# A dynamic convolution ahead of an FFN: one PSUM quadrant per head in the conv, with the last two heads spread by DMA

## The chip, the cores and the metric

The kernel runs on one core of a Trainium2 chip. The metric is the device time of one execution in microseconds (us); lower is better. For the kernel before, three runs gave 747.69, 746.68 and 747.04 us, a median of 747.04 us.

## What is computed

`x` has 8 batches of 4096 tokens with 192 channels; `weight_gen` has 8 heads of 7 taps for each token. The softmax of the taps weighs the token and the six before it, head by head (24 channels each). The result goes through an FFN with a squared ReLU: 192 to 2048 to 192.

```python
w = softmax(weight_gen, axis=-1)                    # B, S, H=8, K=7
x_unf = x_pad[:, idx, :].reshape(B, S, K, H, 24)    # token s-6 .. s
y = einsum('bshk,bskhg->bshg', w, x_unf).reshape(B * S, 192)
h = maximum(y @ w_in, 0.0)                          # 192 x 2048
out = (h * h) @ w_out                               # 2048 x 192
```

## The kernel before

**Blocks.** The 32768 tokens are cut into 64 sub-blocks of 512 tokens (`TB`), and these into 33 blocks (`BLOCKS`): two of one sub-block, then 31 of two. The two halves of a block stand in partitions 0 to 63 and 64 to 127 of `y`, so that matmuls of 64 rows for the two halves lie beside each other in the array.

**Softmax (class `Softmax`).** ACT does the exponentials (step E, L217). DVE sums, inverts and scales them in pieces of eight rows, or six for a last piece (step S: L224, L231, L239), into `v_first` or `v_big`. From there the weights go to rows `wr`, either by DMAs within SBUF on SP and POOL in turn (`move_rows`, `wr_load_sbuf`, L330) or through DRAM (`store` L253, `wr_load`). `TIMES` and the rule beside it say in which block and ahead of which unit each piece is done. From block 4 to block 26 every block has a piece ahead of its last unit, u15; every fourth has another ahead of u9.

**Bands (`st_bands`, L348, step B).** DVE multiplies `wr` by a mask into `bd`, a banded matrix for each head: 128 input tokens by up to 104 output tokens. In steady blocks the two sub-blocks' bands stand ahead of u1 and u5; in blocks 4 to 6 they stand ahead of u7 and u9, or u5 and u9.

**Conv (`st_conv`, step C).** The conv of block j+1 runs within block j. For five token tiles of a sub-block, a piece of `x` (128 tokens by up to 32 channels) is the stationary operand and `bd` of one head the moving one. The 192 channels are six groups of 32 (`quads`), two to a slot `k`; a half has two column groups of 32 in PSUM. A group of 32 channels covers parts of two heads (24 channels each), so it takes two matmuls: all 32 columns with the later head, then the first 8, 16 or 24 again with the earlier head. That makes 3 slots x 2 x 5 tiles x 2 halves x 2 groups = 120 matmuls for a block of two. Two ACT copies (L432), of 1024 and 512 columns, take the two PSUM tiles `yp` to `y` in f16.

**FFN.** A unit u (`st_unit`, 16 in a block) is six h matmuls (L446), a ReLU on ACT into `t1` (L455) and a square on DVE into `g` (L458). The weights `w_i` lie in SBUF twice: as loaded, and with the halves of 64 rows exchanged. A step M (`st_mm2`, L480) is half of a quarter of the second matmul of the block before: M1 of a block uses g0 to g7 and M2 uses g8 to g15 of the block before, both for its first quarter. After every second M, ACT and DVE add the two halves of `o` into `o_sb` (L494, L496), and SP stores it.

**Order.** It is written out by hand. Each engine runs its instructions in program order. Blocks 0 to 3 have plans of their own, the others follow `steady`: eight M, sixteen u and one C. What has a due time (E, S, B, L) is put ahead of its unit. After the conv of block j+1, POOL issues the loads of `x` for block j+2 (`x_load`, L290, L294, L300), into the two buffers that the conv has just read. `h` of a unit and `yp` share three PSUM buffers of two banks (`ps_h`); `t1` has five buffers, `g` 28, `y` two.

Of the kernel before, what the change touches and what calls it, by code (L numbers as in the profile page):

```python
# [9 lines left out]
def kernel(  # L10
# [26 lines left out]
    nc = tc.nc  # L37
    f32 = mybir.dt.float32
    f16 = mybir.dt.float16

    B, S, D = x.shape
    H, KK = weight_gen.shape[2], weight_gen.shape[3]
    Dff = moe_w_in.shape[1]
    Dm = moe_w_out.shape[1]
    HK = H * KK
    HP = H // 2

    P = 128
    TB = 512
    NBB = S // TB  # L50
    NSUB = B * NBB
    BLOCKS = [(0, 1), (1, 1)] + [(n, 2) for n in range(2, NSUB, 2)]
# [6 lines left out]
    RT = 64  # L59
    NK = D // RT  # L60

    NT = 5
    STEP = 104
    BASE = -24
    starts = [BASE + STEP * i for i in range(NT)]
    bounds = [0, 104, 208, 312, 416, TB]
# [5 lines left out]
    const = ctx.enter_context(tc.tile_pool(name="const", bufs=1))  # L72
# [6 lines left out]
    p_y = ctx.enter_context(tc.tile_pool(name="p_y", bufs=2))  # L79
# [4 lines left out]
    ps_h = ctx.enter_context(tc.tile_pool(name="ps_h", bufs=3, space=bass.MemoryType.PSUM))  # L84
# [3 lines left out]
    WQ = 2  # L88
    NQ = Dff // WQ
    w_i = const.tile([P, WQ, 2, NQ + NQ // 2], f16, name="w_i")  # L90
    w_o = const.tile([P, NF, Dm], f16, name="w_o")
    mask = const.tile([P, P, 2], f16, name="mask")
    swap = const.tile([P, P], f16, name="swap")
    FIRST = 8
    PARTS = {0: (8, 8, 8, 8), 1: (8, 8, 16), 2: (16, 16)}
    v_big = const.tile([P, R + 2 * HALO, HP, SL, 2], f16, name="v_big")
    v_first = [
        const.tile([P, FIRST + 2 * HALO, HP, SL, 2], f16, name=f"v_first{i}") for i in (0, 1)
    ]
# [47 lines left out]
                )  # L147
            nc.scalar.copy(out=w_i[:, q, 1, a:b], in_=pt[:, 0 : b - a])

    def w_in_chunk(fc, slot, half):  # L150

        q, f = divmod(fc, NQ // P)
        if slot < 2:
            part, col = slot, f * P
        else:
            second, f = divmod(f, NQ // P // 2)
            part, col = int(second != half), NQ + f * P
        return w_i[RT * half : RT * (half + 1), q, part, col : col + P]
# [10 lines left out]
    class Softmax:  # L169
# [10 lines left out]
        def load(self, eng):  # L180
            r, rh = self.r, self.rh
            self.wg = wg = self.tile(p_wg, p_wg, "wg", HK, "wg8").rearrange(
                "p (r h k) -> p r h k", h=H, k=KK
# [4 lines left out]
            def src(first, count, parts):  # L188
                return bass.AP(
                    tensor=base.tensor, offset=base.offset + first * HK,  # L190
                    ap=[[r * HK, parts], [1, count * HK]],
                )
# [12 lines left out]
        def exp(self, lo, hi):  # L205

            if lo == 0:
                self.ex = self.tile(p_one, p_one, "ex", HK, "ex8").rearrange(
                    "p (r g k e) -> p r g k e", g=HP, k=KK, e=2
                )  # L210
# [57 lines left out]
    x_t, wr_t, bd_t, yp_t, y_t, g_t, h_t, t1_t, o_t, o_sb_t = ({} for _ in range(10))  # L268

    def rows(ap2d, t0, width):  # L270

        return bass.AP(
            tensor=ap2d.tensor, offset=ap2d.offset + t0 * width,
            ap=[[width, P], [STEP * width, NT], [1, width]],
        )
# [5 lines left out]
    def tile_start(j, i):  # L281

        t1 = (j % NBB + 1) * TB
        return TB - P if i == NT - 1 and t1 in ends(j // NBB) else starts[i]
# [17 lines left out]
    def x_load(j):  # L302
        x_t[j] = p_x.tile([P, NT, D], f16, name="xt")
        block_load(j, x_t[j], x[j // NBB], D, nc.gpsimd)

    def x_load_f32(j):
        x_st[j] = p_one.tile([P, (R + HALO) * HK], f32, name="x_st", tag="ex")
        block_load(
# [51 lines left out]
            op=AluOp.mult,  # L360
        )

    G = D // H
    quads = []
    for q in range(D // 32):
        ha, hb = (32 * q) // G, (32 * q + 31) // G
# [3 lines left out]
    def conv_pieces(j):  # L370
# [18 lines left out]
        else:  # L389
            for pair in zip(*halves):  # L390
                for later in (True, False):
                    for k in range(NK):
                        for s, i, half, a, b, base in pair:
                            for q in (2 * k, 2 * k + 1):
                                yield later, s, i, q, half, a, b, base

    def st_conv(j):

        n = BLOCKS[j][1]
        th = n * TB // 2  # L400
        per = 1024 // th
        y = p_y.tile([P, NK, TB], f16, name="y")
        y_t[j] = y
        yps = [
            ps_h.tile([P, 2 * TB], f32, name="yp", tag="h") for _ in range(-(-NK // per))
        ]
        for later, s, i, q, half, a, b, base in conv_pieces(j):
            lo = bounds[i]
            hi = lo + (STEP if tile_start(s, i) == starts[i] else bounds[i + 1] - lo)
            _, ha, hb, pre = quads[q]  # L410
            m, h = (32, hb) if later else (pre, ha)
            bd = bd_t[s][:, H * lo : H * hi].rearrange("p (g c e) -> p g e c", g=HP, e=2)
            p0 = RT * half + 32 * (q % 2)
            k = q // 2
            col = th * (k % per) - base
            nc.tensor.matmul(  # L416
                out=yps[k // per][p0 : p0 + m, col + a : col + b],
                lhsT=x_t[s][:, i, 32 * q : 32 * q + m],
                rhs=bd[:, h // 2, h % 2, a - lo : b - lo],
                start=True,  # L420
                stop=True,
                skip_group_check=True,
                tile_position=(0, p0),
            )
        for n, yp in enumerate(yps):
            k0, k1 = n * per, min((n + 1) * per, NK)

            copies = ((k0, k1, nc.scalar.copy),)
            if j == 0:
                copies = ((0, 2, nc.scalar.copy), (2, NK, nc.vector.tensor_copy))  # L430
            for a, b, copy in copies:
                copy(  # L432
                    out=y[:, a:b, 0:th],
                    in_=yp[:, (a - k0) * th : (b - k0) * th].rearrange("p (k c) -> p k c", c=th),
                )

    def st_unit(j, u):

        th = BLOCKS[j][1] * TB // 2
        per = TB // th  # L440
        h = ps_h.tile([P, 2, TB], f32, name="h", tag="h")
        for jj in range(per):
            for slot in range(NK):
                for half, r0 in enumerate((0, RT)):
                    k = slot ^ half if slot < 2 else slot
                    nc.tensor.matmul(  # L446
                        out=h[:, half, jj * th : (jj + 1) * th],
                        lhsT=w_in_chunk(u * per + jj, slot, half),
                        rhs=y_t[j][r0 : r0 + RT, k, 0:th],
                        start=(jj == 0 and slot == 0), stop=(slot == NK - 1),  # L450
                        skip_group_check=True,
                        tile_position=(r0, 0),
                    )
        t1 = p_t1.tile([P, 2, TB], f16, name="t1")
        nc.scalar.activation(out=t1, in_=h, func=ActF.Relu)  # L455
        g = p_g.tile([P, 2, TB], f16, name="g")
        g_t[(j, u)] = g
        nc.vector.tensor_tensor(out=g, in0=t1, in1=t1, op=AluOp.mult)  # L458
# [56 lines left out]
    with nc.allow_low_precision("fp16 matmul pipeline"), tc.manual_schedule():  # L515
# [26 lines left out]
        def spin(n):  # L542
# [3 lines left out]
        s0, s1, s2 = parts[:3]  # L546
# [5 lines left out]
        w_st = [  # L552
            p_wg.tile([P, (R + HALO) * HK], f32, name="w_st", tag="wg")[:, 0 : NQ + NQ // 2]
            for q in (0, 1)
# [23 lines left out]
        for q in range(4):  # L578
# [4 lines left out]

        steady = "MuMuuu" * 3 + "MuuuMCu"
        plans = {
# [4 lines left out]
        }  # L592


# [28 lines left out]
        for n, s in enumerate(parts[4:], 4):  # L623
            b, f = s.b, s.fb
            k = n - min(m for m, p in enumerate(parts) if p.b == b)
# [8 lines left out]
        for j in range(len(plans), NBLK - 1):  # L634
            a = BLOCKS[j + 1][0]
# [4 lines left out]
        for j in range(len(plans), NBLK):  # L640
            plan, u = [], 0
# [55 lines left out]
        for j in range(NBLK):  # L697
            if j + 2 < NBLK:
                load_rows(j + 2)
            u = 0  # L700
            for step in plans[j].split():
                kind, n = step[0], int(step[1:] or 0)
                if kind == "u":
                    st_unit(j, u)
                    u += 1
                elif kind == "M":
                    next(mm2)
                elif kind == "C" and j + 1 < NBLK:
                    st_conv(j + 1)
                    if j == 0:  # L710
                        x_load(3)
                    elif j + 2 < NBLK:
                        for k in range(BLOCKS[j + 2][0], sum(BLOCKS[j + 2])):
                            x_load(k)
                elif kind == "E":
                    parts[n].exp(*next(parts[n].exps))
                elif kind == "S":
                    soft(parts[n])
                elif kind == "B":
                    st_bands(n)  # L720
                elif kind == "L":
                    parts[n].load(nc.sync)
                elif kind == "X":
                    x_cast(n, nc.vector.tensor_copy)


        j = NBLK - 1
# [44 lines left out]
```

The softmax here doesn't subtract the row's maximum and nothing guards it: scores larger than these inputs give would overflow.

## Time and profile before

| what | value |
|---|---|
| three runs | 747.69, 746.68, 747.04 us; median 747.04 us |
| the profiled execution: span from first to last instruction | 746.6 us (0.4 us under the median of the runs) |
| its own time outside the span | not given by the page; taken as that 0.4 us |
| granted TensorE clock over the span | 1.000 |
| h matmuls (L446), one | 370 ns mean, 3168 of them |
| o matmuls (L480), one | 243 ns mean, 8032 of them |
| conv matmuls (L416), one | 208 ns mean, 3864 of them |
| ReLU (L455), one | 1026 ns, 512 of them |
| square (L458), one | 687 ns, 512 of them |

A row of the page's groups gives line, engine, operation, operands, count, busy time and the mean of one. Matmuls overlap, so the mean of one is longer than the distance from one to the next; distances between starts in the timeline are what counts. The chain is followed back from the last instruction to whatever released it. A wait names the engine that idled and what ended it.

### The profile page before, as it was taken

What the parts mean: (1) busy time and instruction counts of PE and PEld (TensorE: products, weight loads), DVE (VectorE), ACT (ScalarE), POOL (GpSimd) and SP (SyncE); (2) the same over time, 40 slices, a digit from 0 to 9 for tenths busy, and PEclk for the clock granted to TensorE, in tenths of its full rate; (3) what the DMA queues carried; (4) which work ended last, traced back from release to release, by engine and by line L of the source; (5) the groups of instructions that cost most, each with busy time, mean ns of one, the idle gap of its engine ahead of it and who ended that gap; (6) DMA issues with size and microseconds to landing.
All of it is one profiled execution on the core that took longest, in us unless ns stands there. A gap on an engine that the chain in (4) does not pass through costs nothing.

```text
span 746.6 us, 33289 instructions
## 1 busy us (share of the span) xinstructions
PE 738.7 (99%) x15106; PEld 556.1 (74%) x15106; DVE 621.7 (83%) x1002; ACT 624.4 (84%) x755; POOL 89.3 (12%) x130
## 2 busy tenths in 40 slices
PE   8999999999999999999999999999999999999998
PEld 4767777777777778777877777777778777777787
DVE  5999998998889888887889888898888987677853
ACT  4998888898888888888888888888888888888884
POOL 7322220101101100011000110001100011000000
PEclk9999999999999999999999999999999999999999
DMA  7745444436554234643245442265341354432312
GB/s 214 121 97 119 80 86 99 99 72 139 94 118 80 73 59 80 139 79 73 40 80 139 94 72 56 48 139 108 59 80 46 59 108 80 60 70 52 53 46 65
DMA packets 122169, 64.81 MB, mean 87 GB/s; under 512 B 83849, under 2 KB 118636, under 8 KB 121516
## 3 DMA queue, kind: packets, MB, share of 16 engines
q1 hardware_dynamic: 77708, 45.66, 22.3%
q0 software_dynamic: 44176, 16.93, 20.5%
q8 instruction: 118, 1.93, 1.1%
q14 instruction: 23, 0.19, 0.1%
q10 hardware_dynamic: 144, 0.10, 0.0%
HBM read 48.61 MB, written 28.70 MB: 104 GB/s over the span
## 4 chain that ended last, share of the span: by engine, by line
PE 91%; DVE 4%; DMA 2%; ACT 2%; issue 1%; DVEq 0%; ACTq 0%; SPq 0%
PE o L480 43%; PE h L446 42%; PE yp L416 6%; DVE bd L348 2%; DVE g L458 1%; ACT t L455 1%; DMA vd<-v_big 1%; DMA wr<-v_first 1%; DMA wg<-in_weight_gen_dram 0%; DVE v_big L239 0%; ACT ex L217 0%; DVE o_sb L496 0%; DVE ssum L224 0%; DVE rcp L231 0%; DVE v_first L239 0%
## 5 line engine op out<-in xcount | busy, mean ns | idle before, releaser
L455 ACT ACTIVATE t<-h 128x1024 f16<-128x1024 f32 x512 | 496.7, 1026 | 64.5 <-PE h L446 63.9
L458 DVE TENSOR_TENSOR g<-t 128x1024 f16<-128x1024 f16 x512 | 334.1, 687 | 99.1 <-ACT t L455 96.4
L480 PEld LDWEIGHTS <-g 64*128 64x128 f16 (+1 forms) x8032 | 352.5, 94 | 54.2 <-issue 3.8
L480 PE MATMUL o<-w_o,g 64*128 64x192 f16 (+1 forms) x8032 | 385.4, 243 | 0.2
L446 PE MATMUL h<-y,w_i 64*128 64x512 f16 (+1 forms) x3168 | 380.3, 370 | 1.9 <-ACT t L455 0.8
L446 PEld LDWEIGHTS <-w_i 64*128 64x128 f16 x3168 | 162.5, 94 | 117.5 <-issue 5.2
L348 DVE TENSOR_TENSOR bd<-wr,mask 128x4160 f16<-128x4160 f16 (+3 forms) x89 | 149.3, 1701 | 4.2 <-DMA wr<-v_first 4.2
L300 POOL DMA_DIRECT2D xt<-in_x_dram x62 | 51.6, 836 | 445.6 <-PE yp L416 422.7
L494 ACT COPY o_sb<-o 128x384 f32<-128x384 f32 x129 | 62.2, 482 | 33.7 <-PE o L480 33.7
L496 DVE TENSOR_TENSOR o_sb<-o,o_sb 128x384 f32<-128x384 f32 x123 | 68.2, 554 | 8.2 <-ACT o_sb L494 5.6
L432 ACT CAST y<-yp 128x1024 f16<-128x1024 f32 (+1 forms) x64 | 47.9, 799 | 15.1 <-PE yp L416 15.0
L416 PE MATMUL yp<-bd,xt 128*32 128x104 f16 (+8 forms) x3864 | 52.0, 208 | 0.7 <-DVE bd L348 0.3
L416 PEld LDWEIGHTS <-xt 128*32 128x32 f16 (+3 forms) x3864 | 46.2, 92 | 7.1 <-issue 6.4
L239 DVE TENSOR_TENSOR v_big<-ex,rcp 128x112 f16<-128x112 f32 (+1 forms) x136 | 27.3, 264 | 2.1 <-DMA vd<-v_big 0.9
L217 ACT ACTIVATE ex<-wg 128x448 f32<-128x448 f32 (+2 forms) x44 | 27.2, 618 | 2.1 <-DMA wg<-in_weight_gen_dram 2.1
L224 DVE TENSOR_REDUCE ssum<-ex 128x64 f32<-128x448 f32 (+2 forms) x44 | 26.1, 593 | 2.6 <-ACT ex L217 2.6
L231 DVE RECIPROCAL rcp<-ssum 128x64 f32<-128x64 f32 (+2 forms) x44 | 23.7, 539 | 1.5
L290 POOL DMA_DIRECT2D xt<-in_x_dram x7 | 3.8, 548 | 137.1 <-PE yp L416 137.1
L330 POOL DMA_DIRECT2D wr<-v_first x31 | 16.8, 559 | 16.1 <-DVE v_first L239 15.9
L544 PE MATMUL wp<-warm 128*128 128x512 f16 x39 | 10.7, 440 | 1.3 <-DVE warm L536 1.3
L544 PEld LDWEIGHTS <-warm 128*128 128x128 f16 x39 | 4.2, 111 | 7.1 <-issue 2.6
L239 DVE TENSOR_TENSOR v_first<-ex,rcp 128x112 f16<-128x112 f32 (+1 forms) x48 | 9.1, 255 | 0.3
(25 smaller groups left out, 28.7 us busy)
## 6 DMA issues: line engine op xcount, KB each, us to landing
out_dram<-o_sb SPq DMA_DIRECT2D x63, 384.0 KB, 3.0
xt<-in_x_dram POOLq DMA_DIRECT2D x42, 240.0 KB, 6.2
wg<-in_weight_gen_dram SPq DMA_DIRECT2D x4, 1064.0 KB, 8.3
xt<-in_x_dram POOLq DMA_DIRECT2D x20, 192.0 KB, 5.4
wr<-vd SPq DMA_DIRECT2D x38, 80.0 KB, 3.9
vd<-v_big SPq DMA_DIRECT2D x5, 512.0 KB, 5.5
wg<-in_weight_gen_dram SPq DMA_DIRECT2D x5, 392.0 KB
wg<-in_weight_gen_dram SPq DMA_DIRECT2D x3, 616.0 KB, 4.5
```

The costliest lines, as they stand in the source:

```text
L217: nc.scalar.activation(out=self.ex[:, lo:hi].rearrange("p r g k e -> p (r g) k e"), in_=self.wg[:, lo:hi].rearrange("p r (g e) k -> p (r g ...
L239: eng.tensor_tensor(out=bass.AP(tensor=v.tensor, offset=v.offset + lo * H * SL + lo % SL * 2 + g * SL * 2, ap=[list(v.ap[0]), [H * SL + 2, ...
L300: eng.dma_start(out=dst[:, first:last], in_=ap)
L348: nc.vector.tensor_tensor(out=bd_t[j][:, H * lo : H * (lo + len(tiles) * n)].rearrange("p (g m c) -> p g m c", g=shape[1], c=2 * SL), in0= ...
L416: nc.tensor.matmul(out=yps[k // per][p0 : p0 + m, col + a : col + b], lhsT=x_t[s][:, i, 32 * q : 32 * q + m], rhs=bd[:, h // 2, h % 2, a - ...
L432: copy(out=y[:, a:b, 0:th], in_=yp[:, (a - k0) * th : (b - k0) * th].rearrange("p (k c) -> p k c", c=th),)
L446: nc.tensor.matmul(out=h[:, half, jj * th : (jj + 1) * th], lhsT=w_in_chunk(u * per + jj, slot, half), rhs=y_t[j][r0 : r0 + RT, k, 0:th], ...
L455: nc.scalar.activation(out=t1, in_=h, func=ActF.Relu)
L458: nc.vector.tensor_tensor(out=g, in0=t1, in1=t1, op=AluOp.mult)
L480: nc.tensor.matmul(out=oo[:, cc * Dm : (cc + 1) * Dm], lhsT=g[r0 : r0 + n, cc * P : (cc + 1) * P], rhs=w_o[r0 : r0 + n, fc, :], start=(fc ...
L494: nc.scalar.copy(out=o_sb, in_=o[0][:, c])
L496: nc.vector.tensor_tensor(out=o_sb, in0=o[1][:, c], in1=o_sb, op=AluOp.add)
```

## The change

From block 4 on, `st_conv` goes to a new function, `st_conv_spread`. Each head has a column group of 32 of its own: heads 0 to 5 in slots 0 to 2, heads 6 and 7 in a fourth slot. All weights have 32 columns; the eight beyond a head's 24 are channels of a neighbour that are not wanted there. A matmul per head suffices: 4 slots x 5 tiles x 2 halves x 2 = 80. The slots are computed in the order 3, 2, then 0, 1, each pair in one `yp`, copied by ACT with 1024 columns. Then four DMAs on SP, one for each group of 32 partitions, take the 24 rows of the fourth slot into the eight unused rows of each of the first three slots. The rows of `y` thereby come in another order, and the FFN's first weights are loaded a second time in that order, as `w_p`, by 18 DMAs on POOL during block 0. Units of blocks from 4 on use `w_p`. The conv stands earlier in the plan of block 3 and of every later block.

```diff
+    G = D // H
+    SPREAD = H - 2
+    FIRST_SPREAD = 4
...
+    w_p = const.tile([P, WQ, 2, NQ + NQ // 2], f16, name="w_p")
...
+    def load_w_spread():
+
+        def rows(head, k=None):
+            a = moe_w_in[G * head : G * (head + 1)]
+            return a if k is None else a.rearrange("(r k) c -> k r c", k=NK)[k]
+
+        for e in (0, 1):
+            for k in range(NK):
+                for a, n, src in (
+                    (0, G, rows(2 * k + e)), (G, RT // 2 - G, rows(SPREAD + e, k))
+                ):
+                    if k < 2:
+                        p0 = RT * k + 32 * e + a
+                        nc.gpsimd.dma_start(
+                            out=w_p[p0 : p0 + n, :, 0, 0:NQ],
+                            in_=src.rearrange("r (q c) -> r q c", q=WQ),
+                        )
+                    else:
+                        for half in (0, 1):
+                            p0 = RT * half + 32 * e + a
+                            nc.gpsimd.dma_start(
+                                out=w_p[p0 : p0 + n, :, 0, NQ:],
+                                in_=src.rearrange("r (q h c) -> h r q c", q=WQ, h=2)[half],
+                            )
+        for r0, r1 in ((0, RT), (RT, 0)):
+            nc.gpsimd.dma_start(out=w_p[r0 : r0 + RT, :, 1], in_=w_p[r1 : r1 + RT, :, 0])
...
+    def st_conv_spread(j):
+
+        s0, n = BLOCKS[j]
+        y = p_y.tile([P, NK + 1, TB], f16, name="y")
+        y_t[j] = y
+        for ks in ((NK, NK - 1), (0, 1)):
+            yp = ps_h.tile([P, 2, TB], f32, name="yp", tag="h")
+            k0 = min(ks)
+            for k in ks:
+                for i in range(NT):
+                    a, b = bounds[i], bounds[i + 1]
+                    for half in (0, 1):
...
+                        for e in (0, 1):
+                            head = 2 * k + e
+                            p0 = RT * half + 32 * e
+                            c0 = min(G * head, D - 32)
+                            nc.tensor.matmul(
+                                out=yp[p0 : p0 + 32, k - k0, a:b],
+                                lhsT=x_t[s][:, i, c0 : c0 + 32],
+                                rhs=bd[:, head // 2, e, 0 : b - a],
+                                start=True,
+                                stop=True,
+                                skip_group_check=True,
+                                tile_position=(0, p0),
+                            )
+            nc.scalar.copy(out=y[:, k0 : k0 + 2], in_=yp)
+        for p0 in range(0, P, 32):
+            head = SPREAD + p0 // 32 % 2
+            r0 = p0 + G * head - min(G * head, D - 32)
+            nc.sync.dma_start(out=y[p0 + G : p0 + 32, 0:NK], in_=y[r0 : r0 + G, NK])
+
     def st_conv(j):
 
+        if j >= FIRST_SPREAD:
+            return st_conv_spread(j)
...
+        w = w_p if j >= FIRST_SPREAD else w_i
...
-                        lhsT=w_in_chunk(u * per + jj, slot, half),
+                        lhsT=w_in_chunk(w, u * per + jj, slot, half),
...
-        steady = "MuMuuu" * 3 + "MuuuMCu"
+        steady = "MuMuuu" * 2 + "MuMuu" + "MCuu" + "Muuu"
...
-            3: "L5 L6 M S3 u u u M u u u u M u M B6 E4 u u u M M B7 u u u E4 M u M C S4 u",
+            3: "L5 L6 M S3 u u u M u u u u M u M B6 E4 u u u M M B7 u u C u E4 M u M S4 u",
...
                     st_conv(j + 1)
                     if j == 0:
                         x_load(3)
+                        load_w_spread()
```

More of the change, by code (lines that the diff above doesn't have):

```diff
@@ L148, in cross_w_in_by_pe, with w_in_chunk @@
             nc.scalar.copy(out=w_i[:, q, 1, a:b], in_=pt[:, 0 : b - a])
-    def w_in_chunk(fc, slot, half):
+    def load_w_spread():
[22 more added lines that the diff above has]
+            nc.gpsimd.dma_start(out=w_p[r0 : r0 + RT, :, 1], in_=w_p[r1 : r1 + RT, :, 0])
+    def w_in_chunk(w_i, fc, slot, half):
         q, f = divmod(fc, NQ // P)
@@ L361, in st_band @@
         )
-    G = D // H
     quads = []
@@ L395, in conv_pieces @@
                                 yield later, s, i, q, half, a, b, base
+    def st_conv_spread(j):
[9 more added lines that the diff above has]
+                    for half in (0, 1):
+                        s = s0 + half
+                        hi = a + (STEP if tile_start(s, i) == starts[i] else b - a)
+                        bd = bd_t[s][:, H * a : H * hi].rearrange(
+                            "p (g c e) -> p g e c", g=HP, e=2
+                        )
[11 more added lines that the diff above has]
+                                tile_position=(0, p0),
+                            )
+            nc.scalar.copy(out=y[:, k0 : k0 + 2], in_=yp)
[3 more added lines that the diff above has]
+            nc.sync.dma_start(out=y[p0 + G : p0 + 32, 0:NK], in_=y[r0 : r0 + G, NK])
     def st_conv(j):
+        if j >= FIRST_SPREAD:
+            return st_conv_spread(j)
         n = BLOCKS[j][1]
```

## The prediction

> **What bounds the kernel now.** I read the page first (busy shares, then the chain), then the timeline around one conv, then the waits, then windows from conv to conv.
>
> ```profile
> PE 738.7 (99%) x15106; PEld 556.1 (74%) x15106; DVE 621.7 (83%) x1002; ACT 624.4 (84%) x755; POOL 89.3 (12%) x130
> ...
> PE 91%; DVE 4%; DMA 2%; ACT 2%; issue 1%; DVEq 0%; ACTq 0%; SPq 0%
> ```
>
> TensorE (PE) is busy throughout and holds 91% of the chain; from about 145 us on, the windows from conv to conv are 22.5 to 22.9 us each, wholly PE, with DVE at 18.5 to 22.0 us and ACT at 19.1 to 20.0 us. So a matmul taken out is time gained, unless PE is then made to wait. One conv and what follows it (start, duration, engine):
>
> ```profile
> 415.97 1.43 PEld L416 LDWEIGHTS <-xt 128*32 128x32 f16 x120 [0.16 <-issue]
> 415.97 1.59 PE L416 MATMUL yp<-bd,xt 128*32 128x104 f16 x120
> ...
> 416.35 0.69 DVE L458 TENSOR_TENSOR g<-t 128x1024 f16<-128x1024 f16 x1 [0.22 <-ACT t L455]
> ...
> 417.15 1.50 ACT L432 CAST y<-yp 128x1024 f16<-128x1024 f32 x2 [0.46 <-PE yp L416]
> 417.43 0.49 DVE L224 TENSOR_REDUCE ssum<-ex 128x48 f32<-128x336 f32 x1
> ...
> 417.50 0.82 PE L446 MATMUL h<-y,w_i 64*128 64x512 f16 x6
> ...
> 418.15 1.48 PE L480 MATMUL o<-w_o,g 64*128 64x192 f16 x32
> 418.44 0.71 DVE L239 TENSOR_TENSOR v_big<-ex,rcp 128x84 f16<-128x84 f32 x4
> 418.54 1.04 ACT L455 ACTIVATE t<-h 128x1024 f16<-128x1024 f32 x1
> ...
> 419.47 0.81 PE L446 MATMUL h<-y,w_i 64*128 64x512 f16 x6
> 419.61 0.69 DVE L458 TENSOR_TENSOR g<-t 128x1024 f16<-128x1024 f16 x1 [0.46 <-ACT t L455]
> ...
> 420.12 1.48 PE L480 MATMUL o<-w_o,g 64*128 64x192 f16 x32
> ```
>
> From starts: conv 1.53 us (415.97 to 417.50), a unit u 0.65 us (six h matmuls), a half quarter M 1.32 us (418.15 to 419.47). What matters is the DVE: between the squares g14 (416.35) and g15 (419.61) stands a softmax piece S (417.43 on). It is free there, since M, conv and u15 give it time. The second M after it (420.12) needs g15 for its last eighth, at 420.12 + 7/8 of 1.32 = 421.27; g15 ended at 420.30, so the slack is about 1.0 us.
>
> [...] 1.43 us for 30 groups of four is 47.7 ns a group. [...] The 16 KB copies within SBUF land in 2.0 to 2.5 us in quiet windows, in 3.3 to 4.0 us beside loads of x.
>
> **The change part by part.**
>
> *Matmuls.* 29 convs (blocks 4 to 32) go from 120 to 80 matmuls. 40 x 1.43/120 = 0.477 us each, 13.8 us in all. If cost went by weight columns (120 averaging 24, against 80 of 32) only 0.17 us would go; but quarter-microsecond windows across the conv show 40, 40, 39, 37 matmuls in flight through stretches of wide and narrow weights, so I take 0.477.
>
> *ACT.* The second copy grows from 512 to 1024 columns: about 0.4 us a block against 2.5 us or more of idle ACT. Free by itself; its delay is in the walk below.
>
> *The conv's place.* Steady order was "... M7 u12 u13 u14 M8 C S u15 | M1 u0 M2" and is "M7 C u11 u12 M8 u13 u14 S u15 | M1 u0 M2" (S belongs to u15 in the plan; the order built from the changed kernel has g13, g14, S, g15 on DVE, and the last weight loads of M2 wait for DVE). Walk, with C at 0 and no wait on PE: conv to 1.05; u11 1.05, u12 1.70, M8 2.34, u13 3.66, u14 4.31, u15 4.95, M1 5.60, u0 6.92, M2 7.57, so g15 is due at 7.57 + 1.15 = 8.73. ACT: the copies are ready 0.27 after their last matmul, 0.71 and 1.62 (pitch 0.91, from three relus in 2.85 us); relu11 2.53, relu12 3.44, output copy 4.35 (pitch 0.43), relu13 4.78, relu14 5.69 to 6.72. DVE: g14 6.74, S at 7.35, g15 after 1.98 us of S (410.53 to 412.51 in the trace) at 9.33, done 10.02. PE waits 10.05 - 8.73 = about 1.35 us. A six-row piece takes 0.3 less: 1.05. With no ACT backlog relu14 starts 0.53 earlier, the low end, 0.8; if DVE comes one square (0.6) late it is 1.95, the high end. Behind the waiting weight load stands all of PE's queue. S sits at u15 in every block from 4 to 26: 17 with eight-row pieces, 6 with six: 17 x 1.35 + 6 x 1.05 = 29.3 us; block 3 adds 0.2.
>
> *The y DMAs.* Four on SP, behind the second copy (ends 2.63). Issues take 0.43 us at a pitch of 0.55: last issued at about 4.35. They run beside the x loads that POOL issues when conv ends. With 3.3 to 4.0 us to land: 7.65 to 8.35, against u0 at 6.92. In blocks 4 to 26 that wait (0.7 to 1.4) lies in front of the g15 wait and uses it up: not added. In 27 to 30, without S, it stands alone: 4 x 1.0 = 4.0 us (0 to 9). Block 31 loads no x: nothing. Behind them on SP are output stores and wr loads that come later anyway.
>
> *The bands.* The conv now comes three to four units after the last band in blocks 3 to 6 where bands are issued late.
>
> ```profile
> 71.11 2.11 PE L446 MATMUL h<-y,w_i 64*128 64x512 f16 x18
> ...
> 72.30 2.35 DVE L348 TENSOR_TENSOR bd<-wr,mask 128x3328 f16<-128x3328 f16 x2
> ```
>
> ```profile
> 137.78 2.11 PE L446 MATMUL h<-y,w_i 64*128 64x512 f16 x18
> ...
> 139.89 2.31 DVE L348 TENSOR_TENSOR bd<-wr,mask 128x4160 f16<-128x4160 f16 x1
> ```
>
> Block 3: C at 71.11 + 2 x 0.65 = 72.4, band done 74.65: 2.2 us. Block 6: C at 137.78 + 1.29 + 1.32 = 140.4, band done 142.2: 1.8. Likewise block 4 1.9 (band 94.54 to 96.9), block 5 0.9. Sum 6.8; DVE was near full in blocks 4 and 5 (21.4 of 22.9, 22.2 of 22.7 us), so part is the same wait as at the block's end: I take 5 (2 to 7).
>
> *Loading w_p.* 18 DMAs on POOL after 29.0 us.
>
> ```profile
> 28.22 0.83 POOL L300 DMA_DIRECT2D xt<-in_x_dram  x1
> 36.12 0.86 POOL L300 DMA_DIRECT2D xt<-in_x_dram  x1 [7.06 <-PE yp L416]
> ...
> 41.06 2.73 POOL L330 DMA_DIRECT2D wr<-v_first  x5 [2.77 <-DVE v_first L239]
> ```
>
> Each issue costs 0.55 to 0.85 us; in the built order each also waits for the DMA eight before it, and the last two for all sixteen. With 4 to 5 us to land (x: 3.6 to 5.3 there) the two go at about 43, so the x load moves from 36 to 44 and the five wr moves from 41 to about 47, landing near 50. The next band (45.84 now) waits for those moves on DVE, the squares stand behind it, and PE runs out after five t1 and three h buffers, at 53. I work out 3 to 5 us and take 4 (0 to 6).
>
> Sum against the profiled span: 746.6 - 13.8 + 29.3 + 0.2 + 4.0 + 5 + 4 = 775.3. The median of the runs shown (747.04) lies 0.4 above that span: **775.7 us**.
>
> **Rivals.** (1) *Gain kept, faster*: S doesn't hold g15 up. It decides once the wait at the block's end is under 0.48 us: if g14 comes 0.9 us earlier than in my walk, or M2 needs g15 that much later. For it: DVE is idle 17% of the time. Against it: the idle time lies before g14, and the queue is in order. Then 746.6 - 13.8 + about 4 + 0.4 = 737. (2) *The y DMAs come late*: they share queues with the x loads, beside which wr loads took 5.1 to 6.3 us (80 KB in small rows). At 5.0 us they land at 9.35 and u0 waits 2.4 us in 27 blocks: 746.6 - 13.8 + 65 + 9 + 0.4 = 807. Against it: only 24 KB in 1 KB rows. (3) *Start and bands hidden*: 775.7 - 9 = 767, inside the likeliest case's own range.
>
> **How the numbers follow.** Likeliest case (with 3) 0.75, its own range 760 to 793; late y 0.14; gain kept 0.09; ends cancelling 0.02. Low end: waits of 0.8 us in 23 blocks and half of the rest gives 757; high end reaches most of rival 2: 803. About 0.2% is what a measurement of this kernel tells from no change. Faster 0.09, same 0.02, slower 0.89.
>
> **What would show it.** Right: 80 matmuls in about 1.05 us per conv; PE idle 1 us or more per block up to block 26, at M2's last weight loads put down to g, or at u0 put down to DMA y; blocks of 23.1 to 23.5 us; from block 27 shorter ones; a DVE wait on wr moves near 45 us. Wrong: blocks at 22.1 us (rival 1), or u0 waiting over 2 us on y (rival 2), or convs well over 1.05 us.

## The result, and the profile after

Four runs of the changed kernel gave 790.2 to 793.7 us, a median of 791.21 us; four runs of the kernel before beside them gave a median of 747.37 us. The ratio is 1.058 (95% interval 1.055 to 1.061): slower by 44 us, where 28 to 29 us were forecast. It lies in the forecast's range of 757 to 803 us, nearer to its upper end. The profiled execution spans 791.9 us.

The same two lines of the page, busy shares and chain:

```profile
PE 748.9 (95%) x13946; PEld 561.3 (71%) x13946; DVE 622.2 (79%) x1002; ACT 634.4 (80%) x755; POOL 99.9 (13%) x148
...
PE 58%; DMA 14%; DVE 10%; ACT 8%; issue 4%; SPq 4%; POOL 1%; DVEq 0%; POOLq 0%; ACTq 0%
```

The 1160 matmuls are gone (15106 to 13946), and TensorE, which held 91% of the chain, holds 58%: DMA, DVE, ACT and SP's issues have stepped into it. Who waits for what in the whole execution (engine, line, what it waited for: us in total, times, longest):

```profile
PEld L515 <- DMA y<-y: 25.6, 39, 2.2
...
PE h L515 <- DMA y<-y: 22.5, 31, 1.9
...
DVE bd L379 <- DMA wr<-v_first: 9.4, 2, 5.8
...
PE o L549 <- DVE o_sb L565: 3.7, 10, 0.9
...
PE yp L448 <- DVE bd L379: 2.4, 4, 1.5
POOL w_p L179 <- DMA w_p<-in_moe_w_in_dram: 2.4, 1, 2.4
...
PEld L549 <- DVE g L527: 1.5, 7, 0.3
```

PE and PEld wait side by side, so their lines aren't added. What stands out is the y DMA, with 22 to 26 us; the g wait, which the prediction made the main loss, hardly shows. Both waits lie at the end of a block, as the timeline around one conv tells (start, duration, engine):

```profile
417.04 1.11 PE L448 MATMUL yp<-bd,xt 128*32 128x104 f16 x80
...
417.75 1.93 ACT L457 CAST y<-yp 128x1024 f16<-128x1024 f32 x2 [0.65 <-PE yp L448]
...
418.09 1.55 PE L515 MATMUL h<-y,w_p 64*128 64x512 f16 x12
...
419.71 2.82 SPq L461 DMA_DIRECT2D y<-y  x4
...
421.75 2.91 ACT L524 ACTIVATE t<-h 128x1024 f16<-128x1024 f32 x3
...
423.78 0.69 DVE L527 TENSOR_TENSOR g<-t 128x1024 f16<-128x1024 f16 x1 [0.22 <-ACT t L524]
424.38 0.61 DVE L255 TENSOR_REDUCE ssum<-ex 128x64 f32<-128x448 f32 x1
...
424.93 1.14 PE L515 MATMUL h<-y,w_p 64*128 64x512 f16 x6 [0.69 <-DMA y<-y]
...
425.70 1.75 PE L549 MATMUL o<-w_o,g 64*128 64x192 f16 x32
...
426.37 1.49 DVE L527 TENSOR_TENSOR g<-t 128x1024 f16<-128x1024 f16 x2
```

From start to start the conv takes 1.05 us (417.04 to 418.09; 1.53 before). The four y DMAs are issued from 419.71 on, the last from about 421.9. u0 waits for them until 424.93, 7.9 us after the conv's start. On DVE the softmax piece (from 424.38) stands between g14 and g15, and g15 starts at 426.37, though its ReLU, the third of those from 421.75 on, had ended at 424.66. M2 (425.70) needs it, and takes 1.75 instead of 1.50 us. So the y wait comes first and uses up nearly all of the g15 wait behind it. The next conv starts at 440.47, a block of 23.43 us.

At the last boundary no x is loaded, and u0 doesn't wait:

```profile
753.36 2.82 SPq L461 DMA_DIRECT2D y<-y  x4
...
757.70 0.85 PE L515 MATMUL h<-y,w_p 64*128 64x512 f16 x6
```

And in the worst block, at 638 us, TensorE waited 2.5 us for y, in two waits:

```profile
637.82 0.37 PE L515 MATMUL h<-y,w_p 64*128 64x512 f16 x1 [0.59 <-DMA y<-y]
...
640.09 0.82 PE L515 MATMUL h<-y,w_p 64*128 64x512 f16 x5 [1.90 <-DMA y<-y]
```

There the first load of x, too, was issued later than in the block shown above (the first line is that block's, the second the worst one's):

```profile
418.48 1.73 POOL L331 DMA_DIRECT2D xt<-in_x_dram  x2 [21.29 <-PE yp L448]
...
632.11 0.86 POOL L331 DMA_DIRECT2D xt<-in_x_dram  x1 [22.81 <-PE h L515]
```

From the conv's start that is 2.1 us instead of 1.4. By the trace's DMA records the last packet of x starts 7.7 us after the conv's start instead of 6.7, and the last one of y 9.0 instead of 7.1.

That block costs more than its waits, since the granted clock falls behind them. In windows of 2 us (span, PE busy, PEld, DVE, ACT, POOL, granted clock, DMA share, GB/s):

```profile
636.00:638.00 2.00, 1.41 (x31) 1.09 (x26) 1.74 (x4) 1.64 (x2) 0.00 (x0) 1.00 1.36 225
638.00:640.00 2.00, 0.19 (x1) 0.00 (x0) 1.66 (x6) 0.00 (x0) 0.00 (x0) 1.00 0.45 147
640.00:642.00 2.00, 1.91 (x26) 1.68 (x28) 0.00 (x1) 1.02 (x1) 0.00 (x0) 0.73 0.63 256
642.00:644.00 2.00, 2.00 (x22) 1.44 (x19) 0.97 (x2) 0.48 (x1) 0.00 (x0) 0.50 0.11 17
644.00:646.00 2.00, 2.00 (x26) 1.20 (x24) 2.00 (x2) 1.43 (x2) 0.00 (x0) 0.92 0.42 65
```

PE was busy for 1.6 of the 4 us from 636 to 640; then the clock went to one half. Weighed by busy time this loses, as an estimate, 0.27 x 1.91 + 0.50 x 2.00 + 0.08 x 2.00 = 1.7 us. The same happens once more at 56 to 62 us (0.81, 0.50 and 0.84, an estimated 1.4 us of busy time lost).

**Where the 44 us stand.** I cut both traces at the ends of the convs, and took from each interval the same interval of before, less 0.475 us if its conv has the new form. To the interval from conv 3 to conv 4 I added 3.9 us, since two units and two M of block 3 now come behind conv 4 instead of ahead of it. What is left is added time, over a change whose 29 convs each bring their 0.475 us: 59.1 - 13.8 = 45.3 us, the difference of the two spans. Experiments 1 to 4, below, are treated alike:

| us added | to conv 3 | 3 to 4 | 4 to 8 | 8 to 28 | 28 to 32 | sum |
|---|---|---|---|---|---|---|
| predicted | 4.0 | 2.2 | 8.6 | 25.5 | 4.0 | 44.3; 42.5 with the bands cut from 6.8 to 5 |
| after | 5.6 | 2.4 | 12.8 | 33.3 | 5.1 | 59.1 |
| 1: no y DMAs | 5.4 | 3.2 | 10.4 | 26.0 | -0.1 | 44.8 |
| 2: softmax piece at u11 | 5.6 | 2.8 | 13.3 | 31.0 | 4.2 | 57.0 |
| 3: both | 5.2 | 3.1 | 6.2 | 2.1 | -0.1 | 16.6 |
| 4: place of the conv alone | 0.0 | 2.0 | 9.5 | 23.9 | -0.2 | 35.1 |

### The profile page after: what moved, and what is told of

Read it like the earlier page. It is cut to its first block, busy times and chain, and to the rows that moved or that the text cites. A ratio compares the mean times of both kernels' runs of the same rounds, so it can differ in the third digit from the quotient of the medians.

```text
span 791.9 us, 31210 instructions
## 1 busy us (share of the span) xinstructions
PE 748.9 (95%) x13946; PEld 561.3 (71%) x13946; DVE 622.2 (79%) x1002; ACT 634.4 (80%) x755; POOL 99.9 (13%) x148
## 4 chain that ended last, share of the span: by engine, by line
PE 58%; DMA 14%; DVE 10%; ACT 8%; issue 4%; SPq 4%; POOL 1%; DVEq 0%; POOLq 0%; ACTq 0%
PE o L549 30%; PE h L515 25%; DMA y<-y 12%; ACT y L457 5%; SPq L461 4%; DVE bd L379 4%; DVE g L527 3%; PE yp L448 2%; ACT t L524 2%; DMA wr<-v_first 1%; DMA w_p<-in_moe_w_in_dram 1%; DVE o_sb L565 1%; DVE rcp L262 1%; DVE ssum L255 1%; DVE v_big L270 1%
## 5 line engine op out<-in xcount | busy, mean ns | idle before, releaser
L549 PE MATMUL o<-w_o,g 64*128 64x192 f16 (+1 forms) x8032 | 407.7, 243 | 3.8 <-DVE o_sb L565 3.7
L549 PEld LDWEIGHTS <-g 64*128 64x128 f16 (+1 forms) x8032 | 370.2, 94 | 51.8 <-issue 10.0
L515 PE MATMUL h<-y,w_p 64*128 64x512 f16 x2784 | 369.4, 377 | 25.0 <-DMA y<-y 22.5
L515 PEld LDWEIGHTS <-w_p 64*128 64x128 f16 x2784 | 159.4, 94 | 140.2 <-DMA y<-y 25.6
L457 ACT CAST y<-yp 128x1024 f16<-128x1024 f32 x58 | 55.9, 1015 | 24.1 <-PE yp L448 24.1
L515 PE MATMUL h<-y,w_i 64*128 64x256 f16 (+1 forms) x384 | 35.9, 324 | 4.4 <-ACT t L524 3.4
L448 PE MATMUL yp<-bd,xt 128*32 128x104 f16 (+1 forms) x2320 | 34.2, 209 | 2.7 <-DVE bd L379 2.4
L448 PEld LDWEIGHTS <-xt 128*32 128x32 f16 x2320 | 28.8, 95 | 8.5 <-issue 8.5
L515 PEld LDWEIGHTS <-w_i 64*128 64x128 f16 x384 | 19.8, 94 | 14.3 <-issue 7.2
```

The lines of the kernel that those rows point to most:

```text
L448: nc.tensor.matmul(out=yp[p0 : p0 + 32, k - k0, a:b], lhsT=x_t[s][:, i, c0 : c0 + 32], rhs=bd[:, head // 2, e, 0 : b - a], start=True, sto ...
L457: nc.scalar.copy(out=y[:, k0 : k0 + 2], in_=yp)
L515: nc.tensor.matmul(out=h[:, half, jj * th : (jj + 1) * th], lhsT=w_in_chunk(w, u * per + jj, slot, half), rhs=y_t[j][r0 : r0 + RT, k, 0:th ...
L549: nc.tensor.matmul(out=oo[:, cc * Dm : (cc + 1) * Dm], lhsT=g[r0 : r0 + n, cc * P : (cc + 1) * P], rhs=w_o[r0 : r0 + n, fc, :], start=(fc ...
```

## The experiments

Theory A is the prediction's: at the end of a block two waits lie over one another, the y DMAs at u0 and g15 at M2, and either alone costs about as much as both. Theory B: the y DMAs alone make the loss, as the waits of after suggest at first sight. Theory C: g15 behind the softmax piece makes it, and the y wait is only the place where TensorE happens to stand. Experiments 7 to 9 build on what the first six showed; 10 asks what the fallen clock costs. Experiments 1 to 6 are one run each, 7 to 10 the median of four.

**1. Without the y DMAs.**

```diff
         for p0 in range(0, P, 32):
             head = SPREAD + p0 // 32 % 2
             r0 = p0 + G * head - min(G * head, D - 32)
-            nc.sync.dma_start(out=y[p0 + G : p0 + 32, 0:NK], in_=y[r0 : r0 + G, NK])
+            pass
```

> The changed kernel without the four y DMAs: heads 6 and 7 are left out of the FFN's input, the unused rows hold a neighbour's channels. Theory A (two waits lie over each other at each block's end, y at u0 and g15 at M2; either alone costs 1.0 to 1.35 us): the wait moves to g15 in blocks 4 to 26, blocks stay at 23.1 to 23.4 us there and fall to 22.1 us from block 27 on; about 783 us. Theory B (y alone): 22.1 us everywhere, about 757 us. Theory C (g15 alone): no wait at u0 was paid for, about 789 us.

Measured: 778.37 us. The waits between 190 and 640 us:

```profile
PEld L549 <- DVE g L527: 22.7, 19, 1.3
PE o L549 <- DVE g L527: 18.4, 19, 1.1
```

The wait that hardly showed in after stands there in full as soon as y is out of the way. Blocks with a piece of eight rows take 23.42 us, with six 23.09, and those from 28 on, without one, 22.16: the wait costs 1.26 and 0.93 us. B falls: only 13 of 44 us go with the DMAs (A had expected 8).

**2. The softmax piece at u11**, so that g15 isn't behind it.

```diff
-                at(j, u, "S", n)
+                at(j, 11 if u == 15 else u, "S", n)
```

> The changed kernel with the softmax piece ahead of u11 (right behind the conv) where it was ahead of u15; the y DMAs stay. Theory A: only the rest of the wait that M2 showed goes, 0.25 us in 23 blocks; about 785 us, blocks 23.1 us, PE still waits for y at u0. Theory B: 791 us. Theory C: blocks 22.1 us, about 760 us.

Measured: 791.59 us, nothing gained. Between 190 and 640 us:

```profile
PEld L515 <- DMA y<-y: 15.9, 27, 2.0
...
PE h L515 <- DMA y<-y: 12.4, 17, 2.0
```

C falls: with g15 free, the y wait alone holds the time. B's number came out here, though B was refuted by experiment 1. A had expected 785: most blocks are indeed shorter (about 23.2 us instead of 23.4), but behind conv 3 three blocks of this run lost 4 to 6 us each, with the clock at one half in each.

**3. Both together.**

> Both edits: no y DMAs (heads 6 and 7 left out of the FFN's input) and the softmax piece ahead of u11. All theories: blocks of 22.1 us from block 8 on; about 756 us. If blocks stay above 22.3 us a third wait stands behind these two.

Measured: 750.95 us. Alone the two edits bring 13 and 0 us, together 40: this is what two waits over one another look like, and A stands, though 756 us had been expected. From block 8 on the blocks are 22.16 us, against 22.55 before. So 0.39 of the 0.477 us for each conv arrives; u11 and u12 behind the conv take 1.35 us instead of 1.30. The rest of the loss lies ahead of conv 8 (5.2 + 3.1 + 6.2 us). There, between 50 and 165 us, PE still waits for bands, and in M for the sum `o_sb` on DVE:

```profile
PE yp L448 <- DVE bd L379: 2.4, 4, 1.5
PE o L549 <- DVE o_sb L565: 2.3, 5, 0.8
```

**4. The conv's place alone**: the kernel before, with the new places of C and nothing else.

```diff
-        steady = "MuMuuu" * 3 + "MuuuMCu"
+        steady = "MuMuuu" * 2 + "MuMuu" + "MCuu" + "Muuu"
...
-            3: "L5 L6 M S3 u u u M u u u u M u M B6 E4 u u u M M B7 u u u E4 M u M C S4 u",
+            3: "L5 L6 M S3 u u u M u u u u M u M B6 E4 u u u M M B7 u u C u E4 M u M S4 u",
```

> The kernel before with the conv's new place alone (120 matmuls, no y DMAs, no w_p). Theory A and C: g15 comes about 1.0 us late at M2 in 23 blocks and the late bands cost some 6 us in blocks 3 to 6: about 777 us, blocks 23.5 us to block 26 and 22.5 us after. Theory B: only the bands, about 753 us.

Measured: 783.26 us. The waits between 190 and 640 us:

```profile
PEld L480 <- DVE g L458: 20.3, 19, 1.3
PE o L480 <- DVE g L458: 16.0, 19, 1.0
```

Blocks with a piece of eight rows take 23.73 us, with six 23.39, and those without one 22.60. So the g15 wait (1.13 and 0.79 us a block) needs neither the new conv nor the DMAs: moving the conv makes it. This edit computes nothing differently and saves no matmul, and alone it costs 35.6 us, 6 more than A had expected: 23.9 us from conv 8 to conv 28 where 20 blocks of 1.0 us were expected, and 11.5 instead of some 9 ahead of that.

**5. Without the load of w_p**: units read `w_i`.

```diff
-        w = w_p if j >= FIRST_SPREAD else w_i
+        w = w_i
...
                         x_load(3)
-                        load_w_spread()
```

> The changed kernel without the 18 DMAs that load w_p; all units use w_i (the rows of y then meet weights in another order, so the output is another). If the load's hold on POOL delays the early wr moves: the 5.6 us that conv 3 comes late go, about 785.5 us, nothing else moves. If the delay had another source: 791 us.

Measured: 786.03 us, 5.2 less. The interval from conv 2 to conv 3 is 19.65 us, as before (19.66), where after has 25.30. In after, PE stands there for 2.63 and 1.35 us (4.0 in all, as forecast), and by the windows the fallen clock takes most of the rest. Here the clock is at 1.0 there, but falls later, behind a single wait of 1.51 us for a band (timeline, then a window of 2 us):

```profile
74.61 1.39 PE L448 MATMUL yp<-bd,xt 128*32 128x104 f16 x78 [1.51 <-DVE bd L379]
...
76.00:78.00 2.00, 2.00 (x19) 1.28 (x20) 0.32 (x1) 2.00 (x3) 1.72 (x3) 0.53 0.21 21
```

In the block that was the worst of after, the first load of x is issued 1.4 us after the conv's start in this run, as in other blocks, and the block takes 23.37 us instead of 26.87.

**6. The x loads behind the y DMAs**, on the kernel of experiment 2: a small copy on POOL that reads what the DMAs write makes POOL issue the loads of x after them.

```diff
+        nc.gpsimd.tensor_copy(out=gate, in_=y[:, 0, 0:1])
...
-                at(j, u, "S", n)
+                at(j, 11 if u == 15 else u, "S", n)
```

> The second edit (softmax piece ahead of u11, so that y alone is the wait) and a GpSimd copy of one column of y ahead of the x loads, so that these start only when the y DMAs have landed. If the x loads' packets hold the y DMAs up (last block, which loads no x, shows no wait): PE's wait at u0 nearly goes, blocks 22.2 to 22.4 us, about 765 us. If the y DMAs are late by their four issues of 0.72 us and their own landing: 23.2 us a block, 790 us.

Measured: 755.73 us, 36 less than experiment 2, with blocks of 22.25 us. That is 9 us below the 765 expected; the blocks up to conv 8 and the single late ones gained as well. At one boundary:

```profile
401.80 2.82 SPq L461 DMA_DIRECT2D y<-y  x4
...
406.10 0.88 PE L516 MATMUL h<-y,w_p 64*128 64x512 f16 x6
406.43 0.18 POOL L462 CAST gate<-y 128x1 f32<-128x1 f16 x1 [19.59 <-DMA y<-y]
406.95 1.73 POOL L331 DMA_DIRECT2D xt<-in_x_dram  x2 [0.34 <-issue]
```

Four issues fill 2.82 us, 0.72 each, so that the last starts at about 403.95; 2.15 us later u0 runs without a wait. In after, with x in flight, it was 3.0 us (421.9 to 424.9). The issues and these 2.15 us fit in ahead of u0; with the x loads beside them they don't. From 422 to 423 us, behind the last issue of a y DMA (421.9), the queue with the x loads (q0) moved 503 packets, and SP's, with y (q1), 5 (packets, MB, share of the engines; the packets are what counts here):

```profile
q0 software_dynamic: 503, 0.19, 157.2%
q1 hardware_dynamic: 5, 0.00, 1.6%
```

Packets of x start from 420.04 to 423.72, and 92 of the 96 of y only after 423.0. A quarter of y's packets had started 6.4 us after the conv's start, where in this experiment it is 4.2 us; for the last one it is 7.1 against 6.4. So y got through for the most part as the x loads ran out; why its packets start so late beside them isn't shown.

**7. Both waits taken away inside the schedule.** The conv goes further ahead of the block's end (y then has two units and an M more), the softmax piece goes from u15 to u9, where a block has two pieces the second to u12, and convs up to block 7 stay as they were before, with `w_p` loaded in block 5.

```diff
-    FIRST_SPREAD = 4
+    FIRST_SPREAD = 8
...
-        steady = "MuMuuu" * 2 + "MuMuu" + "MCuu" + "Muuu"
+        steady = "MuMuuu" * 3 + "MuuuMCu"
+        early = "MuMuuu" * 2 + "MuM" + "CuuMuuMuuu"
...
+            times = [
+                (j, u) if u != 15 or j + 1 < FIRST_SPREAD else (j, 12 if (j, 9) in times else 9)
+                for j, u in times
+            ]
...
-            for step in steady:
+            for step in early if j + 1 >= FIRST_SPREAD else steady:
...
-                        load_w_spread()
...
+                    if j == 5:
+                        load_w_spread()
```

> 80 matmuls per conv from block 8 on. In those plans the conv stands one half quarter and two units earlier than in the change (y then has 8.5 us from the conv's end to u0 where it needs about 7), softmax pieces stand behind the conv, ahead of u9 and u12; blocks up to 7 as before, w_p loaded in block 5. If the two waits and the early part are all there is: 25 convs x 0.475 us = 11.9 us faster than before, about 735.5 us. If a third wait stands behind them: blocks above 22.2 us, 740 us or more.

Measured: 743.65 us (four runs), a ratio to before of 0.994 (0.993 to 0.996): faster than before, but 8 us short of what was expected. Blocks with one softmax piece take 22.15 us; those with a second one ahead of u12 take up to 23.28. The timeline of one of them:

```profile
167.06 0.61 DVE L255 TENSOR_REDUCE ssum<-ex 128x64 f32<-128x448 f32 x1
...
168.29 0.83 DVE L270 TENSOR_TENSOR v_big<-ex,rcp 128x112 f16<-128x112 f32 x4
...
169.65 0.55 DVE L565 TENSOR_TENSOR o_sb<-o,o_sb 128x384 f32<-128x384 f32 x1
...
170.25 1.48 PE L549 MATMUL o<-w_o,g 64*128 64x192 f16 x31 [0.92 <-DVE o_sb L565]
```

This is a third wait: M1 can't overwrite `o` before DVE has added it into `o_sb`, and that addition stands behind the second piece.

**8 and 9. The second piece elsewhere.** In 8 it goes from u12 to u13, behind the addition. In 9 there is none: batches 4 to 7 are cut into pieces of ten rows, so that one a block, ahead of u9, is enough.

```diff
-            return j, {1: 0, 2: 1, 7: 3, 9: 4, 12: 8, 15: 8}[u]
+            return j, {1: 0, 2: 1, 7: 3, 9: 4, 13: 8, 15: 8}[u]
...
-                (j, u) if u != 15 or j + 1 < FIRST_SPREAD else (j, 12 if (j, 9) in times else 9)
+                (j, u) if u != 15 or j + 1 < FIRST_SPREAD else (j, 13 if (j, 9) in times else 9)
```

```diff
-            piece = s.rh if n < 2 else PIECE
+            piece = s.rh if n < 2 else PIECE if s.b < 4 else 10
...
-                (f - 6, 15), (f - 5, 15), (f - 4, 15), (f - 3, 9), (f - 3, 15)
+                (f - 6, 9), (f - 5, 9), (f - 4, 9), (f - 3, 9)
```

> The kernel of the two moved waits, with one change: in the blocks that have two softmax pieces the second stands ahead of u13 instead of u12. If the third wait is M1 held by the output copy o_sb on DVE, which stands behind the second piece, the piece is now behind that copy and the wait of 0.63 to 1.07 us in six to eight blocks goes: 738 to 741 us. If the room in the DVE's queue up to u15 is what is short, the wait only moves, to g15 at M2 of the next block: 743 to 745 us.

> The kernel of the two moved waits, with the second piece taken away altogether: the softmax parts of batches 4 to 7 are cut into pieces of ten rows, so that four pieces, one a block ahead of u9, are enough and no block holds two. Four blocks lose a wait of about 0.78 us: 743.65 - 3.1 = 740.5 us if the wait comes from the second piece. If longer pieces ahead of u9 hold the squares of u9 up instead, each block pays some tenths and the time stays at 743 to 746 us.

Measured: 738.62 us for 8, a ratio of 0.987 (0.986 to 0.989); 740.21 us for 9, a ratio of 0.989 (0.988 to 0.991), before being 748.34 us beside them. Both came out as the third wait foretold. The chain of 8 and its PE waits for DVE between 190 and 640 us:

```profile
PE 92%; DVE 3%; ACT 2%; issue 1%; DMA 1%; DVEq 0%; ACTq 0%
```

```profile
PEld L549 <- DVE g L527: 0.9, 3, 0.5
...
PE o L549 <- DVE o_sb L565: 0.4, 1, 0.4
PE o L549 <- DVE g L527: 0.3, 1, 0.3
```

TensorE holds the chain again, with no y wait left: of the at most 25 x 0.477 = 11.9 us of its 25 new convs, 9.7 us arrive once they are no longer paid for with waits.

**10. The wait in block 2 filled**, on the changed kernel, to see what the fallen clock costs.

```diff
+        if j == 3:
+            for _ in range(6):
+                nc.tensor.matmul(
+                    out=yps[0][:, 0:TB], lhsT=warm[:, 0:P], rhs=warm, start=True, stop=True
+                )
```

> The changed kernel with six matmuls of zeros (128x128 by 128x512, about 0.22 us each) added ahead of the conv of block 3; they write a PSUM tile that the conv overwrites, and lie in its wait of 1.35 us for the second band. In the changed kernel the granted clock falls to 0.5 between 57 and 61 us, behind some 3 us of waiting within six. If the clock falls because TensorE was idle too long, and costs about 1.7 us there (2 us windows at 0.81, 0.50, 0.84), the clock stays at 1.0, the two intervals from the end of conv 2 to that of conv 4 come to 44.1 instead of 45.8 us, and the whole to about 789.5 instead of 791.2 us. If the clock falls for another reason, or the waits alone make up the loss, nothing moves: 45.8 and 791 us.

Measured: 790.89 us; 45.35 us from conv 2 to conv 4, between the two expectations. The clock fell all the same, and earlier:

```profile
52.00:54.00 2.00, 0.35 (x5) 0.22 (x3) 2.00 (x3) 0.15 (x1) 0.00 (x0) 1.00 0.00 0
54.00:56.00 2.00, 1.07 (x6) 0.30 (x5) 2.00 (x4) 2.00 (x3) 0.00 (x0) 0.67 0.00 0
56.00:58.00 2.00, 2.00 (x6) 0.59 (x5) 2.00 (x3) 2.00 (x4) 0.00 (x0) 0.50 0.00 0
58.00:60.00 2.00, 2.00 (x123) 1.57 (x121) 1.93 (x7) 0.65 (x3) 0.00 (x0) 0.98 0.92 241
```

Here the fall began behind the first wait, of 2.58 us, and ahead of the second, so filling the second couldn't keep the clock up. The zeros ran at half clock in the conv's stead (2.25 us; six of this form take 1.3 us at the start of before, 0.216 us each), and the conv at full clock. So the run doesn't give the price of a fall by itself: that stays at the 1.4 to 1.7 us estimated from the windows.

## Why the prediction was right, and where its sizes were off

**Matmuls: right.** The conv takes 1.05 us, as walked, 0.48 less than before, against 0.477; of that 0.39 us arrive in a block without waits (experiment 3).

**The g15 wait: right in place, and nearly in size.** Taken were 1.35 and 1.05 us (the walk's own difference, 10.05 - 8.73, is 1.32); alone (experiment 1) it costs 1.26 and 0.93 us. That its stretch from conv 8 to conv 28 loses 26.0 us against the 25.5 of the sum is in part luck: the waits make up 15 x 1.26 + 5 x 0.93 = 23.6 us of it, and the rest is mostly one block of 24.82 us and the part of each conv's gain that doesn't arrive. It is the conv's new place that makes the wait (experiment 4). That DVE keeps g15 behind the softmax piece, on which the forecast rests, shows in the block at 417 us: 1.71 us from the end of its ReLU to its start (424.66 to 426.37).

**The y DMAs: the step that they "use up" the g15 wait was right, the term too small.** They land 7.9 us after the conv starts, within the 7.65 to 8.35 forecast. But two errors cancelled: the last is issued 4.8 us after, not 4.35 (a pitch of 0.72 us, not 0.55), and it lands 3.0 us later, not 3.3 or more. That the sum came out right is luck. The typical block is 23.43 us, within the 23.1 to 23.5 forecast; block 31 doesn't wait. The term failed where single blocks take 0.5 to 3.4 us more, since y comes later still beside x: with the blocks of six rows, which now cost as much as those of eight, this makes 33.3 us from conv 8 to conv 28 instead of 25.5 (and of the 26.0 without the y DMAs), and 5.1 instead of 4.0 from 28 on. Rival 2 forecast such late DMAs, but in all 27 blocks; and y and the x loads share no queue: in the trace they are in q1 and q0. From the last issue to u0 the runs show at most 2.2 us for the y DMAs where no x load is in flight, against 3.0 us in the block at 417 us.

**Late bands and the first boundaries: too small.** I had walked 6.8 us and cut it to 5, because a full DVE would make it "the same wait as at the block's end". Experiment 3, which has no wait at the block's end, still loses 9.3 us from conv 3 to conv 8. The traces show about 4 us of it at the conv itself, and a second place that the walk didn't have: the band ahead of the `o_sb` addition holds M up. With y and g15 on top, conv 3 to conv 8 costs 15.2 us against 10.8 as walked, 9.0 as taken.

**Loading w_p: 4.0 us of waits, as taken, and 5.2 us in all, by one run.** On POOL the load of x moved from 36.1 to 41.8 us, not 44, and the last wr move is issued at 47.1, as worked out. The difference is mostly the clock, which no step of mine had. In after it falls to 0.50 twice within the blocks, for 3.4 us each (from 57.2 and 640.9 on), both times behind long waits. Ahead of a fall TensorE was idle for 2.58 us in one piece (experiment 10), for 2.4 of 4 us (after, at 638), and once for 1.51 us (experiment 5); what sets it off isn't shown.

**Rival 1, gain kept**, was refuted for this schedule. That 738.62 us in experiment 8 lies near its 737 is no proof of its sum, since that kernel has 25 new convs and not 29, and no losses at the start; it shows that the gain is there once S and the conv stand where g15 and y have time.

The worst block goes with the late issue of its x load: it is the same one in after and in experiments 2 and 10 (26.87, 26.51 and 26.71 us, x issued 2.1 us after the conv's start each time), and an ordinary one in experiment 5 (23.37 us, x at 1.4). Why the load was released later there stays open, and so does why y is late in some other blocks (one of experiment 2 takes 26.38 us with its x load on time).

## What to carry to other kernels

Where two waits end close together, the list of waits names only the first; take away each alone and both together before believing either, and price the pair by the later one. A step that is moved to give a transfer time also moves what stands behind it in each engine's order (in experiment 4 the conv's new place alone made PE wait 1.13 us for g15 in a block with a piece of eight rows): see to the last consumer of every queue at the new place before counting the matmuls saved. Keep bulk loads from being issued just ahead of a small transfer that the bounding engine waits for (experiment 6 took 36 us less than experiment 2).

## What the runs showed of the hardware that I had not expected

A long wait of TensorE can cost more than itself. In the twelve traces, from the first conv on, each of the nine waits of PE of 1.83 us and more was followed by a fall of the granted clock to 0.50 for 3.4 us or longer (by the windows of after an estimated further 1.4 to 1.7 us lost). Of sixteen waits of 1.4 to 1.8 us only three were (1.51 us in experiment 5, 1.54 and 1.66 in experiment 2), so the length of the wait alone doesn't decide. Waits of up to 1.3 us, in nearly every block of experiments 1 and 4 from 190 to 640 us, left the clock at 1.0. And a 24 KB DMA within SBUF occupies SP for 0.67 us at a pitch of 0.72 us, lands in at most 2.2 us with no x load in flight (the last boundary of after, and experiment 6), and typically in 3.0 us with one.
